# Where the second batch's q and k, the small mixing matrices U and V and the first key beacons are handled at the start of a fused attention and mixer kernel

## The chip, the cores and the metric

The kernel runs on one core of one Trainium2 chip, as one launch. The metric is the device time of that launch in microseconds (us), the median of several runs. Five engines work beside each other, each through its own list of instructions in a fixed order: TensorE (PE: matrix products and transposes, written into PSUM), VectorE (DVE), ScalarE (ACT), GpSimd (POOL) and SyncE (SP, which here only issues transfers). Transfers between memory and the core run on 16 DMA engines; the profile calls what POOL issues queue q0 and what SP issues queue q1.

## The reference, cut to what matters

Eight batches (B), eight heads (H), 576 tokens (S), 16 beacons (Nb), 64 numbers a head (D):

```python
k_all = concat([beacon_k, k]);  v_all = concat([beacon_v, v])      # 16 + 576 keys
scores = (q @ k_all.T) / 8, tokens masked causally, beacons never masked
x = softmax(scores) @ v_all                                        # heads side by side: (8, 576, 512)
u = x + (x.T @ U @ V).T                                            # U: 576 x 32, V: 32 x 576
out = u + relu(u @ w_ch1) @ w_ch2                                  # 512 -> 2048 -> 512
```

## The kernel before, in words

Attention is worked through in pairs of heads, four pairs p to a batch, 32 in all. Of each pair, q and k are turned by TensorE (`qkT_units`, lines 272 to 289: transposes into PSUM, line 260 or 266, and copies to `qT` and `kT`, lines 282 and 287), the scores are made in four column groups (`visit`, line 318, with a mask product ahead of it on line 310), ScalarE takes their exponentials (line 324), and `av_unit` (line 345) multiplies them with v; VectorE divides (lines 353 and 354) and writes `xb`. Tokens of q and k are loaded as `st` (line 192), six tokens to a partition on 96 partitions; the 16 key beacons come in on partitions 96 to 111 (lines 189 and 195). `regroup` (lines 245 to 256) copies a pair into a tile `pr`, so that one transpose serves both heads; line 255 copies the beacons beside the tokens.

When the four pairs of a batch are done, `mix_units` makes u: `head` multiplies with U (line 374, copy `qts` on line 380), `most` and `end` add the product with V (lines 410 and 422, from `Vsb` and `Vend`) to x (line 385) and write `uT` (lines 394 and 396). From then on the two big products (`g_unit`, line 449, with w1 in four loads, and `c_unit`, line 465, with w2 in two) are cut into units and slipped in between the steps of the later pairs (`fill`), until they alone are left.

The order of the start is written out by hand, and every engine keeps to it. First comes batch 0: q and k of the first pairs through SP and ACT, the rest through POOL, then `v[0]` in halves of four heads, five transfers each (line 207). Then POOL issues the lower halves (heads 0 to 3) of `k[1]` and `q[1]`, the key beacons of batch 1, the upper half of `v[0]`, and the first quarter of w1 (line 178). The rest stands in `load_rest` (lines 716 to 727), called during pair p = 0 after that turn's two transposing units: U and V are read by SP into one f32 tile `small` (three transfers of U, four of V, lines 157 to 163; a one-column memset on VectorE, line 155, stands ahead of them), POOL issues the upper halves of `k[1]` and `q[1]` and the v beacons, rounds U, V and the end of V to 16 bits (lines 167, 168 and 171), and then issues `v[1]`, the other three quarters of w1 and w2; `load_batch(2)` adds the loads of batch 2 behind them. At p = 3 the loop writes the order by hand as well (lines 750 to 755): the two `av_unit`s, the two transposing units of pair 5, `head`, and the rest of the mixing with two groups of scores (`two`, `three`) between its parts.

Every product goes through one PSUM pool of 8 buffers (line 100) that are handed round in the order of the program. `keep_warm` (line 234) multiplies constants, to keep TensorE busy: 8 products at the start (on `plain`, which lies in `Vsb`), 2 ahead of the first scores, 2 behind them (line 700), 1 further on.

Of the kernel before, what the change touches and what calls it, by code (L numbers as in the profile page):

```python
# [11 lines left out]
F32 = mybir.dt.float32  # L12
# [6 lines left out]
P = 128  # L19
# [11 lines left out]
def kernel(  # L31
# [13 lines left out]
    nc = tc.nc  # L45
    B, H, S, D = q.shape
    Nb = beacon_k.shape[2]
# [17 lines left out]
    TJ = 6  # L65
# [36 lines left out]
    def pst(shape, dtype, name):  # L102
        return psum.tile(shape, dtype, tag="ps", name=name)
# [33 lines left out]

    Vsb = const.tile([P, QM], F16, name="Vsb", tag="Vsb")
    Vend = const.tile([P, NCC, nq[NT - 1]], F16, name="Vend", tag="Vend")
    plain = Vsb[:, 0:P]  # L140
    nc.vector.memset(plain, 1.0)
    ones = const.tile([P, 1], F16, name="ones", tag="ones")
    nc.vector.memset(ones, 1.0)
# [8 lines left out]
    def small_loads():  # L152

        f = utp.tile([P, NT * R + S], F32, name="small", tag="ut")
        nc.vector.memset(f[:, 0:1], 0.0)
        uf, vf = f[:, 0 : NT * R].rearrange("p (j r) -> p j r", r=R), f[:, NT * R :]
        nc.sync.dma_start(out=uf[: nq[0], 0, :], in_=moe_U[0 : nq[0], :])
        nc.sync.dma_start(
            out=uf[:, 1 : NT - 1, :], in_=moe_U[q0[1] : QM, :].rearrange("(j p) r -> p j r", p=P)
        )  # L160
        nc.sync.dma_start(out=uf[:NL, NT - 1, :], in_=moe_U[QM:S, :])
        for cc in range(NCC):
            nc.sync.dma_start(out=vf[ds(R * cc, R), :], in_=moe_V)

        def cast():
            for rr, jj in ((nq[0], slice(0, 1)), (P, slice(1, NT - 1)), (NL, slice(NT - 1, NT))):
                nc.gpsimd.tensor_copy(out=Usb[:rr, jj, :], in_=uf[:rr, jj, :])
            nc.gpsimd.tensor_copy(out=Vsb, in_=vf[:, 0:QM])
            for cc in range(NCC):
                rs = ds(R * cc, R)  # L170
                nc.gpsimd.tensor_copy(out=Vend[rs, cc, :], in_=vf[rs, QM:S])

        return cast

    def emit_w1(i):
        w1r = moe_w_ch1.rearrange("(cc p) f -> p cc f", p=P)
        fs = ds(FF // 4 * i, FF // 4)
        nc.gpsimd.dma_start(out=w1[:, :, fs], in_=w1r[:, :, fs])
# [12 lines left out]
    def token_load(eng, src, dst, hs):  # L191
        eng.dma_start(out=dst[0:TP, hs, :], in_=src[hs].rearrange("h (p j) d -> p h (j d)", j=TJ))  # L192
# [10 lines left out]
    def v_tokens(src, vs, hs, js=range(NT)):  # L203
        dst = by_head(vs)[:, :, hs, 0:D]
        for j in js:
            a = Nb if j == 0 else 0
            nc.gpsimd.dma_start(  # L207
                out=dst[a : a + nq[j], j, :, :], in_=src[hs, ds(q0[j], nq[j]), :].rearrange("h p d -> p h d")
            )
# [5 lines left out]
    def by_token(t):  # L215
        return t.rearrange("p h (j d) -> p j h d", j=TJ)
# [17 lines left out]
    def keep_warm(ps, n, a=ident):  # L234


        w = ps.shape[-1] // P
        for _ in range(n):
            nc.tensor.matmul(
                ps[:, 0 : w * P].rearrange("p (a b) -> p a b", b=P), a,  # L240
                a.rearrange("p (a b) -> p a b", a=1).broadcast_to([P, w, P]),
                start=True, stop=True,
            )

    def regroup(st, c, i, *copies, beacons=None):

        t = pairs.tile([P, TJ, 2, D], F16, name=f"pr{i}", tag=f"pr{i}")
        src = by_token(st[i][:, 2 * c : 2 * c + 2, :])
        w = TJ // len(copies)
        for a, copy in enumerate(copies):  # L250
            js = slice(w * a, w * (a + 1))
            copy(out=t[0:TP, js], in_=src[0:TP, js])
        if i == 0:
            b = beacons if beacons is not None else src
            copies[0](out=t[TP:TB, TJ - 1], in_=b[TP:TB, TJ - 1])
        return t

    def in_pair(pr):

        return [lambda ps, o, n, j, t=t: nc.tensor.transpose(ps[:, ds(o, n)], t[:n, j, :, :], ident[:n, :n]) for t in pr]  # L260

    def by_heads(st, c):

        def turn(ps, o, n, j, t):
            for h in range(2):
                nc.tensor.transpose(  # L266
                    ps[ds(D * h, D), ds(o, n)], t[:n, 2 * c + h, ds(D * j, D)], ident[:n, :n]
                )

        return [lambda ps, o, n, j, t=t: turn(ps, o, n, j, t) for t in st]  # L270

    def qkT_units(turns, qT, kT, c, copies=((nc.vector.tensor_copy,), (nc.vector.tensor_copy,))):

        def one(i, dst, b0):
            ps = pst([P, SK], F16, name="tps")
            for j in range(TJ):
                n = TP + b0 if j == TJ - 1 else TP
                turns[i](ps, TP * j, n, j)
            w = TJ // len(copies[i])
            for a, copy in enumerate(copies[i]):  # L280
                js = slice(w * a, w * (a + 1))
                copy(  # L282
                    out=dst[:, c, b0 : b0 + S].rearrange("x (p j) -> x p j", j=TJ)[:, :, js],
                    in_=ps[:, 0:S].rearrange("x (j p) -> x p j", j=TJ)[:, :, js],
                )
            if b0:
                copies[i][-1](out=dst[:, c, 0:b0], in_=ps[:, S : S + b0])  # L287

        return [lambda: one(1, qT, 0), lambda: one(0, kT, Nb)]
# [318 lines left out]
    def qkT_of(p):  # L608
        b, c = divmod(p, NH2)
        new_qT_of(p)  # L610
        copies = [(act_copy, nc.vector.tensor_copy) if p == 0 else (nc.vector.tensor_copy,)] * 2
        turns = by_heads(Ls[b][0], c)
        for i, t in enumerate(prs.get(p, ())):
            if t is not None:
                turns[i] = in_pair(prs[p])[i]
        return qkT_units(turns, qTs[b], kTs[b % 2], c, copies)

    def scores_of(p):
# [21 lines left out]

    QUOTA = {2: 4}

    IDLE = [8, 2, 1, 0, 2]
    queue = []
    state = {"t": 0}

# [38 lines left out]
    with tc.manual_schedule(engines={ENG.PE, ENG.Activation, ENG.DVE, ENG.SP, ENG.Pool}):  # L685
# [3 lines left out]
            token_load(nc.gpsimd, src, dst, HALVES[1])  # L689
        v_beacon(beacon_v[0], vss[0])  # L690
        v_tokens(v[0], vss[0], HALVES[0])
        prs[0][0] = regroup(first, 0, 0, V, act_copy, beacons=by_token(Ls[0][0][0][:, 0:2, :]))
        keep_warm(pst([P, 512], F32, name="idle"), IDLE[0], plain)
        t0, sc = qkT_of(0), scores_of(0)
        for u in t0:
# [1 line left out]
        sc[0](IDLE[1])  # L697
        masks = sc[2]
        prs[1] = [None, regroup(first, 1, 1, V)]
        keep_warm(pst([P, 512], F32, name="idle"), IDLE[4])  # L700
        for u in qkT_of(1)[::-1]:
            u()
        clear()
# [7 lines left out]
        token_load(nc.gpsimd, q[1], qt, HALVES[0])  # L711
        key_beacons(nc.gpsimd, beacon_k[1], kt, ALLH)
        v_tokens(v[0], vss[0], HALVES[1])
        emit_w1(0)

        def load_rest():
            cast_small = small_loads()
            token_load(nc.gpsimd, k[1], kt, HALVES[1])
            token_load(nc.gpsimd, q[1], qt, HALVES[1])
            v_beacon(beacon_v[1], vss[1])  # L720
            cast_small()
            v_tokens(v[1], vss[1], HALVES[0])
            emit_w1(1)
            v_tokens(v[1], vss[1], HALVES[1])
            emit_w1(2)
            emit_w1(3)
            emit_w2()

        NP1 = NF * NH2
        for p in range(NP1):  # L730
            b, c = divmod(p, NH2)
            if c == 0 and NF <= b + 1:
                load_batch(b + 1)
            seq = []
            prior = masks
            if p + 2 < NP1:
                seq += [lambda i=i, p=p: qkT_of(p + 2)[i]() for i in range(2)]
            if NH2 + 3 <= p + 3 < NP1:
                seq.append(lambda p=p: regroup_of(p + 3))
            if p + 1 < NP1:  # L740
                one_by_one = sc[3]
                seq.append(sc[1])
                masks = sc[2]
            seq += [prior] + av_of(p)
            sc = []
            if p + 2 < NP1:
                new_qT_of(p + 2)
                sc = scores_of(p + 2)
                seq.append(lambda sc=sc, p=p: sc[0](IDLE[3] if p < NH2 else 0))
            if p == NH2 - 1:  # L750
                two, three = one_by_one
                _, head, (most, end), begin = mix_units(xbs[b], 0, False)
                seq = (
                    seq[-3:-1] + seq[0:2] + [head, two, lambda: begin([0, 1]), three, most, end] + seq[-1:]
                )
            done = 0
            for i, u in enumerate(seq):
                u()
                if p == 0 and i == 1:
                    load_rest()  # L760
                want = FIRST[p] * (i + 1) // len(seq)
                fill(want - done)
                done = want
            if c == NH2 - 1:
                if b == 0:
                    queue.extend([None] * 4)
                    feed(b)
                else:
                    mix(b)
# [146 lines left out]
```

## Time and profile before

| what | value |
|---|---|
| median of 3 runs | 358.02 us (357.6 to 358.52) |
| profiled execution, its own time | 358.65 us |
| its span, first to last instruction | 357.0 us |
| TensorE busy | 348.2 us, 98% |
| VectorE, ScalarE, GpSimd busy | 188.1, 166.1 and 97.4 us |
| mean granted TensorE clock | 0.995 |
| read from memory, written | 37.59 MB, 9.44 MB |

The profiled execution took 358.65 us, of which 357.0 us lie in the span; the 1.65 us around it are the same for any change inside. A busy TensorE is an engine with an instruction in it: where its clock is halved, the same products show longer. All that the change touches lies in the first 35 us of the span, and its transfers reach on to about 62 us.

### The profile page before, as it was taken

What the parts mean: (1) busy time and instruction counts of PE and PEld (TensorE: products, weight loads), DVE (VectorE), ACT (ScalarE), POOL (GpSimd) and SP (SyncE); (2) the same over time, 40 slices, a digit from 0 to 9 for tenths busy, and PEclk for the clock granted to TensorE, in tenths of its full rate; (3) what the DMA queues carried; (4) which work ended last, traced back from release to release, by engine and by line L of the source; (5) the groups of instructions that cost most, each with busy time, mean ns of one, the idle gap of its engine ahead of it and who ended that gap; (6) DMA issues with size and microseconds to landing.
All of it is one profiled execution on the core that took longest, in us unless ns stands there. A gap on an engine that the chain in (4) does not pass through costs nothing.

```text
span 357.0 us, 7830 instructions
## 1 busy us (share of the span) xinstructions
PE 348.2 (98%) x3134; PEld 174.1 (49%) x3134; DVE 188.1 (53%) x485; ACT 166.1 (47%) x356; POOL 97.4 (27%) x139
## 2 busy tenths in 40 slices
PE   7989999999999999999999999999999999999995
PEld 2655455455555444444444444444454444444443
DVE  5758755588986444654465447445745522313311
ACT  4966751478745464467444664556503202401400
POOL 8759613609239028304820500000000000000000
PEclk9989999999999999999999999999999999999999
DMA  8999999999999949996999893142014215115111
GB/s 171 144 177 109 188 204 175 208 173 119 107 96 140 183 98 124 156 198 86 133 147 203 129 138 80 61 101 55 31 61 99 58 59 95 25 59 90 30 55 69
DMA packets 143946, 41.37 MB, mean 116 GB/s; under 512 B 128800, under 2 KB 139296, under 8 KB 143904
## 3 DMA queue, kind: packets, MB, share of 16 engines
q0 software_dynamic: 87408, 18.18, 66.0%
q1 hardware_dynamic: 56272, 22.34, 32.1%
q8 instruction: 26, 0.43, 0.5%
q10 hardware_dynamic: 224, 0.30, 0.3%
q14 instruction: 16, 0.13, 0.1%
HBM read 37.59 MB, written 9.44 MB: 132 GB/s over the span
## 4 chain that ended last, share of the span: by engine, by line
PE 90%; DMA 4%; POOL 2%; DVE 2%; ACT 1%; issue 1%; POOLq 0%
PE gps L449 36%; PE cps L465 34%; PE po L345 8%; PE sps L318 7%; DMA vs<-in_v_dram 2%; DMA st<-in_q_dram 2%; PE tps L260 1%; PE cph L490 1%; PE qtp L374 1%; POOL vs L207 1%; PE ups L385 1%; PE ups L410 1%; POOL st L192 1%; DVE uT L392 1%; ACT expt L324 0%
## 5 line engine op out<-in xcount | busy, mean ns | idle before, releaser
L324 ACT ACTIVATE expt<-sps 128x496 f16<-128x496 f32 (+2 forms) x256 | 111.3, 533 | 63.6 <-PE sps L318 63.5
L449 PE MATMUL gps<-uT,w 128*128 128x512 f16 x576 | 135.4, 379 | 0.0
L465 PE MATMUL cps<-w,gT 128*128 128x512 f16 x560 | 132.7, 379 | 0.0
L453 ACT ACTIVATE gT<-gps 128x512 f16<-128x512 f32 x86 | 51.9, 607 | 95.0 <-PE gps L449 95.0
L449 PEld LDWEIGHTS <-w 128*128 128x128 f16 x576 | 52.0, 98 | 59.3 <-issue 3.2
L465 PEld LDWEIGHTS <-gT 128*128 128x128 f16 x560 | 49.9, 98 | 59.2 <-issue 6.8
L455 DVE TENSOR_SCALAR gT<-gps 128x512 f16<-128x512 f32 x58 | 40.0, 690 | 47.8 <-PE gps L449 46.5
L478 DVE TENSOR_TENSOR ob<-cps,ut 128x512 f32<-128x512 f32 x31 | 21.4, 690 | 49.6 <-PE cps L465 49.2
L345 PEld LDWEIGHTS <-expt 128*128 128x128 f16 (+1 forms) x960 | 37.6, 99 | 17.5 <-issue 3.8
L207 POOL DMA_DIRECT2D vs<-in_v_dram x50 | 39.6, 809 | 15.2 <-DMA w<-in_moe_w_ch_dram 8.4
L345 PE MATMUL po<-vs,expt 128*128 128x65 f16 (+1 forms) x960 | 40.5, 195 | 1.8 <-DMA vs<-in_v_dram 1.4
L318 PE MATMUL sps<-qT,kT 64*128 64x80 f16 (+4 forms) x384 | 35.0, 284 | 0.7 <-DVE kT L287 0.6
L354 DVE TENSOR_TENSOR xb<-po,rec 128x320 f16<-128x320 f32 x64 | 31.5, 492 | 2.2
L295 DVE TENSOR_TENSOR expt<-expt,bigmask 128x512 f16<-128x512 f16 x54 | 22.6, 419 | 11.7 <-ACT expt L324 11.7
L353 DVE RECIPROCAL rec<-po 128x5 f32<-128x5 f32 x64 | 12.0, 187 | 26.3 <-PE po L345 26.2
L318 PEld LDWEIGHTS <-kT 64*128 64x128 f16 x384 | 11.7, 94 | 22.7 <-issue 14.2
L189 POOL DMA_DIRECT2D vs<-in_beacon_v_dram x8 | 4.3, 532 | 59.7 <-PE po L345 59.7
L548 POOL DMA_DIRECT2D st<-in_q_dram x20 | 16.9, 864 | 3.8 <-DMA st<-in_k_dram 2.2
L548 POOL DMA_DIRECT2D st<-in_k_dram x20 | 16.9, 868 | 1.6 <-DMA vs<-in_v_dram 1.1
L392 DVE TENSOR_TENSOR uT<-ups,uT 128x496 f16<-128x496 f32 x20 | 12.1, 667 | 6.9 <-PE ups L410 3.6
L282 DVE COPY qT<-tps 128x576 f16<-128x576 f16 (+1 forms) x16 | 11.8, 736 | 3.9 <-PE tps L260 2.5
L282 DVE COPY kT<-tps 128x576 f16<-128x576 f16 (+1 forms) x16 | 11.7, 732 | 1.9 <-PE tps L266 1.1
(83 smaller groups left out, 142.2 us busy)
## 6 DMA issues: line engine op xcount, KB each, us to landing
out_dram<-ob SPq DMA_DIRECT2D x35, 256.0 KB, 2.2
vs<-in_v_dram POOLq DMA_DIRECT2D x18, 128.0 KB, 7.6
w<-in_moe_w_ch_dram POOLq DMA_DIRECT2D x4, 512.0 KB, 7.8
w<-in_moe_w_ch_dram POOLq DMA_DIRECT2D x2, 1024.0 KB, 13.6
st<-in_k_dram POOLq DMA_DIRECT2D x12, 128.0 KB, 7.5
st<-in_q_dram POOLq DMA_DIRECT2D x12, 128.0 KB, 8.9
st<-in_k_dram POOLq DMA_DIRECT2D x2, 576.0 KB, 13.1
st<-in_q_dram POOLq DMA_DIRECT2D x2, 576.0 KB, 16.0
```

What stands on the lines that cost most here:

```text
L207: nc.gpsimd.dma_start(out=dst[a : a + nq[j], j, :, :], in_=src[hs, ds(q0[j], nq[j]), :].rearrange("h p d -> p h d"))
L282: copy(out=dst[:, c, b0 : b0 + S].rearrange("x (p j) -> x p j", j=TJ)[:, :, js], in_=ps[:, 0:S].rearrange("x (j p) -> x p j", j=TJ)[:, :, js],
L295: nc.vector.tensor_tensor(out=e4, in0=e4, in1=bigmask, op=ALU.min)
L318: nc.tensor.matmul(ps[g, i][:, ds(o, w)], kT[hp, c, ds(P * ch, P)], qT[hp, c, ds(qa, w)], start=not early, stop=True, skip_group_check=early,)
L324: nc.scalar.activation(out=ex[i][:, ds(SLOT * g, gw[g])], in_=ps[g, i][:, 0 : gw[g]], func=AF.Exp, scale=scale)
L345: nc.tensor.matmul(po[:, j, :], ex[0 : nk[c], ds(blk[(c, j)], P)], vs[0 : nk[c], ds(c * H * E + h * E, E)], start=(c == 0), stop=(c == j),)
L354: nc.vector.tensor_tensor(out=xb[:, :, ds(h * D, D)], in0=po[:, :, 0:D], in1=r.broadcast_to([P, NT, D]), op=ALU.mult)
L449: nc.tensor.matmul(g[:, 0:n], w1[:, cc, ts(dc, P)], uT[:, cc, ds(t0, n)], start=(cc == 0), stop=(cc == NCC - 1))
L453: nc.scalar.activation(out=gT["t"][:, dc, 0:n], in_=g[:, 0:n], func=AF.Relu)
L455: nc.vector.tensor_scalar_max(out=gT["t"][:, dc, 0:n], in0=g[:, 0:n], scalar1=0.0)
L465: nc.tensor.matmul(ps[:m, :], gT["t"][:, dc, ds(P * i, m)], w2[:, dc, :], start=(dc == 0), stop=turned and dc == NDC - 1, skip_group_check ...
L548: nc.gpsimd.dma_start(out=dst[a : m[j], j, :, :], in_=src[:, ds(q0[j], nq[j]), :].rearrange("h p d -> p h d"))
```

## The change

It does five things.

1. POOL issues the upper halves of `k[1]` and `q[1]` ahead of the first quarter of w1, outside `load_rest`.
2. `load_rest` is called one pair later, at p = 1. For POOL this alters nothing of the order by itself; the memset that SP's reads of U and V wait for stands one pair later on VectorE. POOL rounds U and V straight away, ahead of the v beacons of batch 1.
3. The four small copies that round the end of V (`cast_end`) leave POOL and are made by VectorE, at p = 3, between the second `av_unit` and the transposing units of pair 5.
4. The key beacons of the first pair are no longer copied beside the tokens: `beacons_apart` turns the 96 tokens as before and the 16 beacons by two small transposes straight from `st`.
5. The two `keep_warm` products of line 700 go, and `plain` lies in `w2` instead of `Vsb`.

```diff
-    plain = Vsb[:, 0:P]
+    plain = w2[:, 0, 0:P]
...
             nc.gpsimd.tensor_copy(out=Vsb, in_=vf[:, 0:QM])
+
+        def cast_end():
             for cc in range(NCC):
                 rs = ds(R * cc, R)
-                nc.gpsimd.tensor_copy(out=Vend[rs, cc, :], in_=vf[rs, QM:S])
-
-        return cast
+                nc.vector.tensor_copy(out=Vend[rs, cc, :], in_=vf[rs, QM:S])
+
+        return cast, cast_end
...
-        if i == 0:
-            b = beacons if beacons is not None else src
-            copies[0](out=t[TP:TB, TJ - 1], in_=b[TP:TB, TJ - 1])
+        if i == 0 and beacons:
+            copies[0](out=t[TP:TB, TJ - 1], in_=src[TP:TB, TJ - 1])
...
+    def beacons_apart(turn, st, c):
+
+        def both(ps, o, n, j):
+            turn(ps, o, TP, j)
+            for h in range(2) if n > TP else ():
+                nc.tensor.transpose(
+                    ps[ds(D * h, D), ds(o + TP, Nb)], st[TP:TB, 2 * c + h, ds(D * j, D)], ident[TP:TB, TP:TB],
+                )
+
+        return both
...
+        if p == 0:
+            turns[0] = beacons_apart(turns[0], Ls[0][0][0], 0)
...
-        keep_warm(pst([P, 512], F32, name="idle"), IDLE[4])
...
         v_tokens(v[0], vss[0], HALVES[1])
+        token_load(nc.gpsimd, k[1], kt, HALVES[1])
+        token_load(nc.gpsimd, q[1], qt, HALVES[1])
         emit_w1(0)
 
         def load_rest():
-            cast_small = small_loads()
-            token_load(nc.gpsimd, k[1], kt, HALVES[1])
-            token_load(nc.gpsimd, q[1], qt, HALVES[1])
+            cast, cast_end = small_loads()
+            cast()
             v_beacon(beacon_v[1], vss[1])
-            cast_small()
             v_tokens(v[1], vss[1], HALVES[0])
             emit_w1(1)
...
             emit_w2()
+            return cast_end
...
-                    seq[-3:-1] + seq[0:2] + [head, two, lambda: begin([0, 1]), three, most, end] + seq[-1:]
+                    seq[-3:-1] + [cast_end] + seq[0:2] + [head, two, lambda: begin([0, 1]), three, most, end] + seq[-1:]
...
-                if p == 0 and i == 1:
-                    load_rest()
+                if p == 1 and i == 1:
+                    cast_end = load_rest()
```

More of the change, by code (lines that the diff above doesn't have):

```diff
@@ L243, in keep_warm, with regroup @@
             )
-    def regroup(st, c, i, *copies, beacons=None):
+    def regroup(st, c, i, *copies, beacons=True):
         t = pairs.tile([P, TJ, 2, D], F16, name=f"pr{i}", tag=f"pr{i}")
@@ L641 @@
     QUOTA = {2: 4}
-    IDLE = [8, 2, 1, 0, 2]
+    IDLE = [8, 2, 1, 0]
     queue = []
@@ L691 @@
         v_tokens(v[0], vss[0], HALVES[0])
-        prs[0][0] = regroup(first, 0, 0, V, act_copy, beacons=by_token(Ls[0][0][0][:, 0:2, :]))
+        prs[0][0] = regroup(first, 0, 0, V, act_copy, beacons=False)
         keep_warm(pst([P, 512], F32, name="idle"), IDLE[0], plain)
```

## The prediction

> **What bounds the kernel now.** The page comes first: PE is busy 98% of the span and fills 90% of the chain that ended last. So the time is PE's work plus PE's stops, and the only long stop is early. The chain in order of time shows it:
>
> ```profile
> PE 90%; DMA 4%; POOL 2%; DVE 2%; ACT 1%; issue 1%; POOLq 0%
> ```
>
> ```profile
> 4.49 6.63 DMA st<-in_q_dram
> ...
> 12.60 2.90 POOL vs L207 x4
> 15.50 6.99 DMA vs<-in_v_dram
> 22.53 1.03 PE po L345 x16
> ```
>
> PE at 22.53 starts on v[0]'s upper half, whose last transfer was issued at 15.50 and took 6.99 us. The table by stage shows the stop and what followed:
>
> ```profile
> 20.00:22.00 2.00, 1.12 (x23) 0.78 (x23) 0.74 (x3) 2.00 (x6) 0.96 (x4) 1.00 1.20 215
> 22.00:24.00 2.00, 1.47 (x22) 1.27 (x23) 1.05 (x4) 0.11 (x1) 0.00 (x0) 0.61 1.29 218
> 24.00:26.00 2.00, 2.00 (x28) 1.22 (x27) 0.47 (x2) 1.42 (x4) 1.27 (x4) 0.53 1.02 149
> 26.00:28.00 2.00, 1.92 (x62) 1.46 (x60) 1.93 (x6) 0.54 (x2) 1.94 (x5) 1.00 0.37 45
> ```
>
> The columns are the stretch, the busy time of PE, PEld, DVE, ACT and POOL, the granted clock, the DMA share and GB/s. After the stop the clock is down (0.61, then 0.53) until about 26. At 26 to 28 the DMA engines, full until then, fall to 45 GB/s: POOL had stood still for V and then rounded it. The timeline has these rows:
>
> ```profile
> 13.68 0.06 DVE L155 MEMSET small<- 128x1 f32 x1
> ...
> 15.14 2.86 SPq L163 DMA_DIRECT2D small<-in_moe_V_dram  x4
> ...
> 18.47 0.68 POOL L192 DMA_DIRECT2D st<-in_k_dram  x1 [1.55 <-DMA st<-in_q_dram]
> ...
> 24.61 0.60 POOL L168 CAST Vsb<-small 128x496 f16<-128x496 f32 x1 [3.43 <-PE sps L318]
> ...
> 25.16 1.17 POOL L171 CAST Vend<-small 32x80 f16<-32x80 f32 x4
> ...
> 26.28 3.59 POOL L207 DMA_DIRECT2D vs<-in_v_dram  x5
> ...
> 29.64 0.39 PE L410 MATMUL ups<-Vsb,qts 32*128 32x496 f16 x4
> ```
>
> The row of Vsb names PE, but the transfer list has V's last transfer issued at 17.58 and landing after:
>
> ```profile
> small<-in_moe_V_dram SPq DMA_DIRECT2D x1, 72.0 KB, 6.9
> ```
>
> 17.58 + 6.9 = 24.5: POOL waited for V. I call V's landing T; before, T = 24.5. Behind it on POOL stand v[1], w1, w2 and batch 2. Its last trace is here, where a copy waits 0.89 for batch 2's key beacons:
>
> ```profile
> 60.96 0.19 DVE L255 COPY pr<-st 16x128 f16<-16x128 f16 x1 [0.89 <-DMA st<-in_beacon_k_dram]
> ```
>
> **The change, part by part.**
>
> *Beacon copy and keep-warm products.* The copy (DVE, 5.90 to 6.41) goes; PE had waited for it and finished the first k at 6.69. Without it the 96-row transposes end by 6.32, plus two small ones at 37 ns (12 of 96 rows took 0.45): 6.4. That is 0.25 earlier for the first exponentials (8.34). The two products are 0.53 of PE (8.45 to 8.98). But ACT runs on without a break to 22.1, so of both only ACT's gap before 10.45 (0.15) and the 0.25 come through: **0.4**. No wait is added: those beacons landed at 1.44 + 4.0 = 5.4. Bounds: 0 (hidden by the wait for v) to 0.8. `plain`'s new place costs nothing: w2 is written from 37 on, the products end at 4.8.
>
> *U and V a slot later.* v[0]'s upper half no longer shares the DMA engines with them. Its last transfer took 7.0; the same transfer of the lower half (issued at 8.67, no U and V beside it) took 5.4. So it lands up to 1.6 sooner (bounds 0 and 1.6), at 20.9, about when PE, 0.4 ahead, wants it. Worth: av of pair 2 then costs 1.09 (the row of pair 1) and not 20.37 to 23.37, 1.9 less; what PE did from 23.37 to 26.3 at half clock (0.59, 0.98, 1.55) costs about 1.0 less at the full clock. With the 0.4, PE ends av of pair 3 at 23.0 and not 26.3: **3.3 won, if nothing is late next.**
>
> *V is late next.* The new memset stands behind pair 3's copies (17.39 before, 17.0 now). V's last issue came 3.9 after the memset, so at 20.9. Latencies of these seven reads were 5.5 to 6.9 with the DMA share above 1; it stays so, as k[1], q[1] and w1 (landed 26.0, 27.4 and 24.7 before) are still to come. So T = 26.4 to 27.8; I take **27.3**, near the upper end because q[1] and w1 are both in flight then. The bounds are wider: 22.5 (a read alone on SP took 3.1 to 4.4 in the first microseconds, less something) and 28.5.
>
> *Who waits for T.* Three chains, each against its row:
>
> - VectorE. `cast_end` waits for T, and behind it in order stand the q and k copies of pair 5 (0.75, 0.75, 0.15) and `qts` (0.28). The four copies have no row on DVE: 0.155 (128x16) to 0.51 (the 16x128 copy, beside POOL) each, so 0.6 to 2.0; I take 0.19, the 80x80 row, 0.75. PSUM's 8 buffers let PE get no further than `three` meanwhile. So L410 comes at T + 0.1 + 0.75 + 1.65 + 0.28 + 0.3 = T + 3.1 = 30.4 (before: 29.64), **0.8 late**.
> - v[1], first half. POOL rounds Vsb (T + 0.1 to T + 0.7), issues the v beacons (0.54) and starts v[1] at T + 1.24; the fifth issue lies 2.92 on and took 2.7 to land: T + 6.9 = 34.2. Its first reader's last product ended at 33.18: with T = 27.3 it ends at about 34.2, **1.0 late**; it breaks even at T = 26.1 (some product time lies behind the landing). The 1.17 of Vend and POOL's place for the v beacons are in this: without them v[1] had started at T + 1.8.
> - Batch 2. The DMA engines are full from 32 to 61, so whatever POOL issues later lands later by as much. v[1] starts at 28.54 for 26.28: 2.26 later; the copy at 60.96 moves with it. Its q and k are done at 62.85 and PE turned them at 63.35, so 0.5 is spare: **1.8 late**. In between w1 and w2 have more room (the second quarter of w1 lands at 36.7, its first product is at 38.66; the last of w2 lands at 54.0, needed at 56.6).
>
> They overlap; the largest sets the end: **+1.8**. The 3.3 is spent in waiting. *k[1] and q[1] ahead of w1* cost nothing: w1's first quarter landed at 24.7, its first product is at 33.0, and 5 us of later landing are covered; if that cover went, PE would stop for what is over. The two were wanted at 31 and had landed at 27.4.
>
> The sum: span 357.0 + 1.8 = 358.8, own time 360.4 for 358.65. The runs' median, 358.02, lies 0.63 below the profiled run, so the prediction is 358.02 + 1.8 = **359.8**.
>
> **A rule that speaks against this.** The DMA engines carried U and V beside POOL's backlog at 5.5 to 6.9 us each. The Trainium skill (DMA: Bandwidth & Descriptors, Queues, rings and completion order) says each engine takes turns between the queues that have work, a packet at a time; by that alone a read from SP need not wait for POOL's backlog. By it V would land as it does unhindered; that is the rival called V early. The trace's latencies of 5.5 to 6.9 us are against it.
>
> **The rivals.**
>
> - *V early (faster).* If V takes the 3.5 of the first reads (3.1 to 4.4), T = 20.9 + 3.5 = 24.4. Then batch 2 is 24.4 + 1.24 - 26.28 - 0.5 = -1.1, the other chains are earlier still: **356.9**; at T = 22.5 it is -3.0, 355.0. It decides from T below 25.5. For it: the early rows, and less v to carry. Against it: the seven latencies, and that k[1], q[1] and w1 are unfinished. I give T below 24.9 two in ten, centre 356.5.
> - *A draw.* T of 24.9 to 26.4, through a share of both: -0.6 to +0.9, about **358.2**.
> - *The clock as well (slower still).* PE in the new order has little from 26.0 (two groups of scores done) to 28.8 (the first copy, which frees a buffer). Before, 1.7 us with 0.3 of work halved the clock for some 3.4. If that comes after 29, the 2.9 between L410 and av of pair 4 grow by up to 1.7: 0.8 + 1.7 = +2.5, **360.5**; with T = 28, 361.2. The Trainium skill (TensorE: Matmul & The Clock Gate, Why this matters for your kernels) bids one avoid idle gaps over about 3 us. By that a gap of 2.8 would cost nothing; the stop of 1.7 in this trace did cost.
> - *It doesn't do what it says.* q[1]'s lower half, not U and V, holds v[0] up, and the stop at 21 stays. Then PE is at cast_end at 26, T is the same, and the time too: **359.8**, with the clock's dip where it was.
>
> **How the numbers follow.** Forecast (with the last rival) 0.5; V early 0.2; draw 0.2; clock as well 0.1. The likeliest gives 359.8. Its own range is T = 26.4 to 27.8 by the batch-2 chain, 358.9 to 360.3, and 2.0 for slow copies carries the VectorE chain to +2.0. The range of 8 in 10 leaves out the lower half of V early and the worst of the clock: **356.3 to 361.4**. A measurement can tell about 0.3% here, 1.07 us. Faster than 356.95: most of V early, 0.16. Within: the draw, the rest of V early and the forecast's lowest T, 0.27. Slower than 359.09: 0.57.
>
> **What would show it.** Right: PE's wait for v[0] at 21 short; VectorE's first 32x80 copy waiting for `small` until about 27; Vsb's row at 27.4; v[1] starting near 28.5; L410 near 30.4; the beacon copy of batch 2 near 63. Wrong: V landing by 25, then all of these come early and the end with them; or the DMA engines falling idle before 26, which would say that V had no backlog to wait for. It is wrong in size if the four copies take over 1.2, or if the clock is low after 26.

## The result, and the profile after

The changed kernel takes **360.28 us** (median of 6 runs, 359.74 to 361.26); the kernel before, run beside it, 357.76 (6 runs, 356.91 to 358.52). The ratio is **1.0078, with a 95% interval of 1.0056 to 1.0100**: slower by 0.8%, 2.5 us by the medians, where 1.8 was forecast. Ratios here are taken over runs within 1.5% of their kernel's fastest, so they can differ a little from the medians.

The profiled execution of the changed kernel took 359.74 us, the shortest of its six, with a span of 358.1 for 357.0. It shows the way in which the time went, but not all of it: 1.1 of some 2.5 us. Lines of code stand up to 14 higher than before (`av_unit` is L357, the first big product L461).

The chain that ended last has changed its make-up:

```profile
PE 81%; DMA 10%; DVE 3%; POOL 2%; SPq 1%; ACT 1%; issue 1%; ACTq 0%; POOLq 0%
```

PE's share falls from 90% to 81%, and DMA's rises from 4% to 10%: transfers now end waits for longer. More than half of that 10% is one transfer, the key beacons of batch 2 (20.49 us); the last part shows that it did not add to the time. The timeline says which waits matter (start, duration, engine and line; in brackets the idle time ahead and what ended it):

```profile
17.52 0.06 DVE L155 MEMSET small<- 128x1 f32 x1
...
18.98 2.56 SPq L163 DMA_DIRECT2D small<-in_moe_V_dram  x4
...
20.55 1.09 PE L357 MATMUL po<-vs,expt 128*128 128x65 f16 x30
...
25.00 0.32 PE L267 MATMUL tps<-ident,st 96*64 96x96 f16 x5 [1.08 <-issue]
...
26.67 0.20 DVE L173 CAST Vend<-small 32x80 f16<-32x80 f32 x1 [0.19 <-DMA small<-in_moe_V_dram]
...
26.80 0.60 POOL L168 CAST Vsb<-small 128x496 f16<-128x496 f32 x1 [1.78 <-DMA small<-in_moe_V_dram]
...
27.87 3.58 POOL L209 DMA_DIRECT2D vs<-in_v_dram  x5
...
29.13 0.60 PE L422 MATMUL ups<-Vsb,qts 32*128 32x496 f16 x4
...
33.04 1.01 PE L357 MATMUL po<-vs,expt 128*128 128x65 f16 x15
...
33.86 1.16 PE L461 MATMUL gps<-uT,w 128*128 128x512 f16 x4
```

In the kernel before, the first big product stood here:

```profile
33.02 1.03 PE L449 MATMUL gps<-uT,w 128*128 128x512 f16 x4
```

The stop of TensorE at 21 is gone: the 30 products of pair 2 take 1.09. But V, read 3.84 us later, lands about 2.2 later, near 26.7 (24.5 before). VectorE's last small copy waits for it, and so does POOL, which starts v[1] at 27.87 for 26.28. The first of the big products comes at 33.86 for 33.02. From there on PE is busy again and nothing is made good. In this trace TensorE never waits for v[1] itself: the row at 33.04, which reads it, has no wait. TensorE even reads V at 29.13, 0.51 ahead of the kernel before (29.64), but then takes 4.73 us to the first big product where it took 3.38.

The table by stage (stretch; busy time of PE, PEld, DVE, ACT and POOL; granted clock; DMA share; GB/s) shows why:

```profile
24.00:26.00 2.00, 1.00 (x31) 0.74 (x33) 0.68 (x3) 0.21 (x1) 0.21 (x1) 1.00 1.09 221
26.00:28.00 2.00, 1.22 (x19) 0.80 (x18) 1.49 (x4) 1.06 (x2) 1.21 (x3) 0.83 0.22 38
28.00:30.00 2.00, 2.00 (x20) 1.20 (x21) 0.80 (x4) 0.82 (x3) 2.00 (x3) 0.50 0.59 38
30.00:32.00 2.00, 2.00 (x30) 1.10 (x29) 1.49 (x4) 1.88 (x5) 2.00 (x4) 0.50 1.15 73
```

TensorE is busy for little more than half of 24 to 28, and runs at half clock from 27.3 to 34.1; before, the half clock stood at 22 to 26. The DMA engines carry 38 GB/s from 26 to 30: POOL, which waits for U and V, issues no transfer between the first quarter of w1 (18.52) and the v beacons (27.34).

### The profile page after: what moved, and what is told of

It reads as the page before. It is cut to its first block, busy times and chain, and to the rows that moved or that the text cites. A ratio compares the mean times of both kernels' runs of the same rounds, so it can differ in the third digit from the quotient of the medians.

```text
span 358.1 us, 7829 instructions
## 1 busy us (share of the span) xinstructions
PE 350.0 (98%) x3134; PEld 175.2 (49%) x3134; DVE 188.5 (53%) x488; ACT 166.4 (46%) x356; POOL 96.3 (27%) x135
## 4 chain that ended last, share of the span: by engine, by line
PE 81%; DMA 10%; DVE 3%; POOL 2%; SPq 1%; ACT 1%; issue 1%; ACTq 0%; POOLq 0%
PE cps L477 32%; PE gps L461 31%; PE sps L330 7%; PE po L357 6%; DMA st<-in_beacon_k_dram 6%; DMA w<-in_moe_w_ch_dram 2%; DMA small<-in_moe_V_dram 2%; PE tps L261 1%; DMA stk<-in_k_dram 1%; POOL vs L209 1%; PE cph L502 1%; ACT expt L336 1%; PE qtp L386 1%; DVE pr L254 1%; PE ups L422 1%; DVE uT L404 1%
## 5 line engine op out<-in xcount | busy, mean ns | idle before, releaser
L461 PE MATMUL gps<-uT,w 128*128 128x512 f16 x576 | 135.5, 380 | 0.0
L461 PEld LDWEIGHTS <-w 128*128 128x128 f16 x576 | 52.1, 98 | 59.4 <-issue 3.4
L357 PEld LDWEIGHTS <-expt 128*128 128x128 f16 (+1 forms) x960 | 36.8, 98 | 15.2 <-issue 1.9
L357 PE MATMUL po<-vs,expt 128*128 128x65 f16 (+1 forms) x960 | 39.6, 195 | 0.2 <-DVE ob L490 0.2
```

The source lines that it names most:

```text
L357: nc.tensor.matmul(po[:, j, :], ex[0 : nk[c], ds(blk[(c, j)], P)], vs[0 : nk[c], ds(c * H * E + h * E, E)], start=(c == 0), stop=(c == j),)
L461: nc.tensor.matmul(g[:, 0:n], w1[:, cc, ts(dc, P)], uT[:, cc, ds(t0, n)], start=(cc == 0), stop=(cc == NCC - 1))
```

## The experiments

Each kernel was timed in 5 rounds beside the kernel before; ratios are to that kernel. Where an edit is given it is made to the changed kernel, unless it says otherwise. All of them compute the whole result.

### Undoing one part at a time

**The slot.** U and V are read at pair 0 again.

```diff
-                if p == 1 and i == 1:
+                if p == 0 and i == 1:
                     cast_end = load_rest()
```

> Theory A (V lands late because its reads wait a slot longer; TensorE then stops at pair 3, the clock halves, and POOL starts v[1] 1.6 us later than before): with the reads of U and V back at pair 0 and all else as changed, V lands near 24.5, v[1] starts near 25.8, and the time is 357.3 to 358.5. Rival 1 (the four copies of V's end hold VectorE up, whenever V lands): 359.5 or more. Rivals 2 (the order of k[1], q[1] and w1) and 3 (the start: no beacon copy, two products fewer, a clock that comes up later): 360.3 as it is.

Measured: 357.99 us, ratio 1.0002 (0.9976 to 1.0028). The slot is the whole loss: undone alone, it takes all of it back. Its trace:

```profile
24.09 1.02 DVE L173 CAST Vend<-small 32x80 f16<-32x80 f32 x4
...
24.85 3.59 POOL L209 DMA_DIRECT2D vs<-in_v_dram  x5
...
25.66 0.32 PE L267 MATMUL tps<-ident,st 96*64 96x96 f16 x5 [1.86 <-issue]
```

VectorE's four copies wait for nothing, and v[1] starts at 24.85, 1.4 ahead of the kernel before. TensorE does not stop at 21 here either. What that wins is lost in a stop of 1.86 with no releaser, after which the clock is halved for some 3.4 us; the first big product is at 32.97, as before the change (33.02).

**The end of V.** It goes back to POOL, behind `Vsb`.

```diff
             nc.gpsimd.tensor_copy(out=Vsb, in_=vf[:, 0:QM])
-
-        def cast_end():
             for cc in range(NCC):
                 rs = ds(R * cc, R)
-                nc.vector.tensor_copy(out=Vend[rs, cc, :], in_=vf[rs, QM:S])
+                nc.gpsimd.tensor_copy(out=Vend[rs, cc, :], in_=vf[rs, QM:S])
+
+        def cast_end():
+            pass
```

> The end of V goes back to POOL, all else as changed. Theory A: v[1] starts 1.2 us later still, 360.3 to 361.5. Rival 1: VectorE is free at pair 3, 358 to 359. Rivals 2 and 3: 360.3.

Measured: 362.58 us, 1.0147 (1.0111 to 1.0183), slower still, and above the range of theory A too: in this trace v[1] starts 1.9 us later than in the changed kernel, not 1.2. The trace shows the link to v[1] in the open (here `av_unit` is L358, the big product L462):

```profile
29.77 3.59 POOL L210 DMA_DIRECT2D vs<-in_v_dram  x5
...
33.59 0.25 PE L358 MATMUL po<-vs,expt 128*128 128x65 f16 x3 [0.92 <-DMA vs<-in_v_dram]
...
34.20 0.28 PE L358 MATMUL po<-vs,expt 128*128 128x65 f16 x4 [0.36 <-DMA vs<-in_v_dram]
...
35.52 0.49 PE L358 MATMUL po<-vs,expt 128*128 128x65 f16 x6 [1.03 <-DMA vs<-in_v_dram]
35.82 1.90 PE L462 MATMUL gps<-uT,w 128*128 128x512 f16 x4
```

VectorE is free, so TensorE reaches pair 4 early, and waits there three times for v[1], block by block. In the same trace the DMA engines move nothing at all at 28 to 30:

```profile
28.00:30.00 2.00, 1.56 (x18) 1.00 0.00 0
```

(stretch, busy PE, clock, DMA share, GB/s). POOL has waited for V until 27.59 and then rounds it, with every further load behind it. Rival 1 falls: moving the end of V to VectorE was the better place for it.

**The order of k[1], q[1] and w1.**

```diff
-        token_load(nc.gpsimd, k[1], kt, HALVES[1])
-        token_load(nc.gpsimd, q[1], qt, HALVES[1])
         emit_w1(0)
...
             cast, cast_end = small_loads()
+            token_load(nc.gpsimd, k[1], kt, HALVES[1])
+            token_load(nc.gpsimd, q[1], qt, HALVES[1])
             cast()
```

> The upper halves of k[1] and q[1] go back behind the first quarter of w1, all else as changed. Theory A: V still lands near 26.7, 359.8 to 360.8. Rival 2: 357.8 to 358.8. Rivals 1 and 3: 360.3.

Measured: 360.75 us, 1.0098 (1.0066 to 1.0129). No gain; the order costs nothing that can be measured, as forecast. Rival 2 falls.

**The start.** The beacon copy and the two constant products come back.

```diff
-        if p == 0:
-            turns[0] = beacons_apart(turns[0], Ls[0][0][0], 0)
...
-        prs[0][0] = regroup(first, 0, 0, V, act_copy, beacons=False)
+        prs[0][0] = regroup(first, 0, 0, V, act_copy, beacons=None)
...
         prs[1] = [None, regroup(first, 1, 1, V)]
+        keep_warm(pst([P, 512], F32, name="idle"), 2)
```

(and in `regroup`, as before, the copy of the beacons).

> The beacon copy and the two keep-warm products come back, all else as changed. Theory A: 359.8 to 360.9. Rival 3: the clock is full before 6 us again and the time 357.8 to 358.8. Rivals 1 and 2: 360.3.

Measured: 361.11 us, 1.0099 (1.0061 to 1.0138). Rival 3 falls. Nor does the new start win anything that shows.

**The slot alone, in the kernel before.** Only the call of `load_rest` is moved, in the kernel before.

```diff
-                if p == 0 and i == 1:
+                if p == 1 and i == 1:
                     load_rest()
```

> The kernel before with nothing changed but load_rest one pair later, so U and V alone are read later. Theory A (the slot is the whole cost): V lands near 28, v[1] starts near 29.8, 360.5 to 363. If it takes the slot and the other edits together: 357.8 to 359.

Measured: 361.98 us, 1.0109 (1.0074 to 1.0143). Without any of the other edits the slot costs as much. So in the kernel before the later slot alone makes the loss, as in the changed kernel undoing it alone takes the loss away. VectorE has none of V's copies here; POOL's queue is enough. v[1] starts at 28.81 in this trace, the first big product is at 34.41.

### By which way a late V costs

**The clock.** Eight constant products stand ahead of the stop at pair 3.

```diff
-            [lambda: visit([2]), lambda: visit([3])],
+            [lambda: visit([2]), lambda idle=0: visit([3], idle)],
...
-    [head, two, lambda: begin([0, 1]), three, most, end]
+    [head, two, lambda: begin([0, 1]), lambda: three(8), most, end]
```

> As changed, with 8 constant products (1.7 us at full clock) ahead of TensorE's stop at pair 3, so that its clock should stay up after 27. Theory A1 (of the late V it is the halved clock that costs): 358.8 to 359.8. Theory A2 (POOL's late start of v[1] sets the end, through batch 2's beacons): 360.0 to 361.0.

Measured: 361.06 us, 1.0086 (1.0055 to 1.0117): no gain, and just above A2's range. Yet the products did what they were for:

```profile
30.00:32.00 2.00, 2.00 (x28) 1.00 0.90 57
32.00:34.00 2.00, 1.77 (x42) 1.00 1.42 88
```

The clock is full where it was halved, and TensorE arrives at pair 4 only to wait for v[1]:

```profile
34.72 0.40 PE L357 MATMUL po<-vs,expt 128*128 128x65 f16 x6 [0.71 <-DMA vs<-in_v_dram]
34.95 1.03 PE L461 MATMUL gps<-uT,w 128*128 128x512 f16 x4
```

So A1 falls as the whole cause: beside so late a v[1], a full clock only brings TensorE to the next wait. With v[1] early it wasn't tried, so what the half clock costs there stays open. A2 named the right queue but, as below, not the right reader.

**VectorE's place alone.** The four copies stand just ahead of the products that read V.

```diff
-    seq[-3:-1] + [cast_end] + seq[0:2] + [head, two, lambda: begin([0, 1]), three, most, end]
+    seq[-3:-1] + seq[0:2] + [head, two, lambda: begin([0, 1]), three, cast_end, most, end]
```

> As changed, but the four copies of V's end stand behind VectorE's other work of pair 3, just ahead of the products that read V. TensorE then goes on at 25 and stops less. If VectorE's place in line costs (the first of the prediction's three chains): 358.5 to 359.5. Theory A2 (POOL): 360.0 to 360.8, for v[1] starts no sooner.

Measured: 362.39 us, 1.0118 (1.0074 to 1.0162): no gain, and above both ranges. VectorE no longer waits with other work behind it, but POOL does, and TensorE's waits for v[1] add up to

```profile
PE po L357 <- DMA vs<-in_v_dram: 2.3, 4, 0.9
```

(us in total, times, longest).

**POOL's place alone.** The lower half of v[1] goes ahead of the rounding.

```diff
-            cast()
             v_beacon(beacon_v[1], vss[1])
             v_tokens(v[1], vss[1], HALVES[0])
+            cast()
```

> As changed, but POOL issues the beacons and the lower half of v[1] ahead of rounding U and V. Theory A2: batch 2 no longer comes late, 358 to 359.3. Theory A1: V lands later still beside v[1], the stop at pair 3 grows, 360.3 to 361.5.

Measured: 360.56 us, 1.0080 (1.0051 to 1.0109): no gain either. v[1] starts at 19.80, and batch 2's beacon copy comes at 60.57, earlier than before the change; so A2, which ran through batch 2, falls. Now VectorE is the one that waits, and TensorE behind it:

```profile
27.01 0.50 DVE L173 CAST Vend<-small 32x80 f16<-32x80 f32 x2 [0.30 <-DMA small<-in_moe_V_dram]
27.43 0.60 POOL L168 CAST Vsb<-small 128x496 f16<-128x496 f32 x1 [2.95 <-DMA small<-in_moe_V_dram]
27.54 0.76 DVE L294 COPY qT<-tps 128x576 f16<-128x576 f16 x1
...
28.35 0.22 PE L322 MATMUL sps<-negmask,identb 128*128 128x128 bf16 x1 [1.87 <-DVE qT L294]
```

The time lies in A1's range, and the clock is halved from 28.6 to 32.0; with v[1] early, the wait and the half clock behind it can't be told apart here.

Two queues wait for V side by side, then. That each hides what freeing the other would give became theory C.

**Both places.** The last two edits together, V still read a slot late.

> As changed, with U and V still read a slot later, but neither queue waits for V with other work behind it: POOL issues the lower half of v[1] ahead of rounding, and VectorE rounds V's end behind its other work of pair 3. If the late V costs only through these two queues (theory C, from the traces so far: the first big product comes 5.6 to 6.1 us after POOL starts v[1], and freeing one queue alone leaves the other): 357.5 to 359. If V's lateness costs by itself, whoever waits (theory D: the product that reads V is late): 360 or more.

Measured: 358.49 us, 1.0023 (0.9990 to 1.0055), against 1.0078 for the changed kernel. Theory C holds: with nothing behind V in either queue, most of the loss is gone although V is no sooner. By the medians 0.74 us is left, which the interval doesn't tell from nothing. The profiled execution of this kernel is one of its longest (360.67 us), with U itself late: TensorE stops for 1.70 with no releaser and waits 1.43 for U, V is rounded at 29.45, and the first big product comes at 34.91. So a late U or V can still cost, as theory D has it; how often it does so here isn't shown.

### Towards a version that beats both

The remaining three read U and V at pair 0 or earlier.

**The slot undone and VectorE's copies late** (the edits of the first and of `cast_end`).

> U and V read at pair 0 again, and V's end rounded behind VectorE's other work; the rest as changed. Theory C: POOL starts v[1] near 25, TensorE's stop at pair 3 shrinks, 355.8 to 357.2. If the stop is TensorE's own (theory E: the earlier trace showed 1.9 us with no releaser ahead of the pair's last five transposes): 357.5 to 358.3, as with the slot alone undone.

Measured: 357.51 us, 0.9988 (0.9955 to 1.0020). The profiled execution has a span of 354.9, its clock full from 5.3 on and the first big product at 30.75, 2.3 ahead of the kernel before; over twelve runs (355.59 to 359.83) that does not come every time. The median lies at the lower edge of theory E's range, the profiled execution (356.66) in theory C's; between the two it stays unclear.

**With v[1] ahead of the rounding as well.**

> The same with the lower half of v[1] issued ahead of rounding. Theory C: 355.3 to 357. Theory E: 357.5 to 358.3. If v[1] beside V slows V down by over 2 us: 358 to 359.5.

Measured: 357.91 us, 0.9988 (0.9956 to 1.0020). No more than the one above, and in theory E's range, not C's. But in this trace TensorE waits 1.7 for v[0] at 20, which neither theory has.

**U and V earlier still.** The reads start ahead of batch 1's loads.

```diff
+        cast, cast_end = small_loads()
         Ls[1] = qk_tiles()
         (kt, qt), _ = Ls[1]
...
         def load_rest():
-            cast, cast_end = small_loads()
             cast()
```

(on top of the slot undone and the copies late; POOL rounds V at its place in line).

> As the second, with the reads of U and V earlier still, from about 11.4, ahead of batch 1. V lands near 22, but beside the lower halves of k[1] and q[1] and the upper half of v[0]. Theory C: if TensorE then waits for v[0] at 21 as before the change, 357 to 358.5; if not, 355.5 to 357.

Measured: 356.89 us, 0.9973 (0.9942 to 1.0003). It has the lowest median of all, 0.86 under the 357.75 of the kernel before, but its interval still takes in 1: a lead that these runs don't prove. The memset stands at 10.05, V is rounded at 20.80 without a wait, and v[1] starts at 21.87. TensorE doesn't wait for v[0] at 21, but now it waits for its lower half, 1.2 us in all up to 14.6, and the clock is halved from 14.1 to 17.5: in part the earlier reads have only moved the stop forward.

## Why the prediction was right, point by point

- **V is late next: right.** Forecast: memset at 17.0, last issue at 20.9, V at 27.3. Measured: 17.52, 20.48 and about 26.7 in the changed kernel; its four reads took 6.1 to 6.4 us (5.5 to 6.9 forecast). In the other kernels with the late slot VectorE's or POOL's last wait for V ended between 26.9 and 29.5. The rule of the Trainium skill (DMA: Bandwidth & Descriptors, Queues, rings and completion order), by which engines take turns between queues, did not save V: 72 KB took over 6 us beside POOL's backlog. V early and the draw didn't come.
- **U: no term, and not always free.** POOL waits for U first, and `head` reads it. In the trace of the changed kernel TensorE doesn't wait for it, but in five of the eight others with the late slot it does, for 0.4 to 1.6 us. No run tells U's part from V's.
- **The stop at 21: right.** v[0]'s last transfer was issued at 15.31 and took 5.4 us: 20.7, forecast 20.9, and TensorE didn't wait. It ended pair 3's products near 23.4 (forecast 23.0). The gain was real, and was spent by the next wait.
- **The start: wrong, 0.4 forecast and nothing seen.** The first exponential came at 8.32 (8.34 before), and ACT's unbroken run at 10.77 (10.45). In this execution TensorE ran at half speed there, up to about 10 us (the four products of the first scores took 0.98 us, 0.58 before); the copy's 0.25 doesn't show through. Putting the old start back didn't change the time.
- **VectorE's chain: the wait came, its lateness didn't.** The copies took 0.19 to 0.20 each, as taken; L410's successor, L422, came at 29.13 with V at 26.7: V + 2.5, forecast V + 3.1. That the first three copies were done as their own transfers landed made it 0.6 shorter. That is 0.51 ahead of the kernel before, where 0.8 late was forecast: what the wait cost in this trace came behind it, through the clock (below).
- **v[1]'s chain: right, too small.** The forecast had v[1] start at V + 1.24; it was 27.87 with V at 26.7. In the seven kernels with the late slot where POOL waited, the first big product came 5.6 to 6.1 after that start (5.99 here, 6.05, 5.75, 6.12, 6.06, 5.98, 5.60). With the forecast's own 28.54 this gives 34.5, 1.5 late and not 1.0: the products behind the last landing were counted too low. In five of the seven TensorE is seen to wait for v[1]. In the changed kernel's own trace and in that of the old order it isn't; there the half clock, to 34.1 and 34.9, brought it no sooner, so that these two fit the 6 us by chance as far as is known.
- **Batch 2's chain: the step that failed.** It was called the largest, at +1.8, and it cost nothing. Its copy did come late, even by 2.37 for the 2.26 forecast:

```profile
63.33 0.19 DVE L256 COPY pr<-st 16x128 f16<-16x128 f16 x1 [2.17 <-DMA st<-in_beacon_k_dram]
...
66.79 0.58 PE L330 MATMUL sps<-qT,kT 64*128 64x496 f16 x4
```

  In the kernel before:

```profile
61.18 0.88 DVE L252 COPY pr<-st 96x768 f16<-96x768 f16 x2
...
63.35 0.42 PE L260 MATMUL tps<-ident,pr 96*128 96x96 f16 x6
...
65.83 0.58 PE L318 MATMUL sps<-qT,kT 64*128 64x496 f16 x4
```

  But the scores behind it came at 66.79 for 65.83: 0.96 late, hardly more than the 0.84 that TensorE had brought along from 33.86, and it was 0.97 late already at its last product ahead of pair 8 that needs none of this (L485, 63.23 for 62.26). The mistake lay in the spare time: the copies up to 62.85 were taken for pair 8's, and the later ones are pair 9's. Pair 8's were done near 61.5 and read at 63.35, so 1.8 was spare and not 0.5. The chain of waits in the profile after runs through this very transfer (20.49 us of it): a chain with no slack left, not one that added time.
- **The clock as well: came, and is part of it.** It was halved from 27.3 to 34.1 in this trace, and here it made the lateness of the first big product: 4.73 us from the product that reads V, for 3.38. Kept full beside a late v[1], the time was the same, since TensorE then waited for v[1]; so the half clock alone isn't the cause, and its share in the changed kernel stays open. Where the half clock reached beyond the first big product it cost more: in the kernel before with the late slot, 1.39 late at the first big product became 2.96 at the scores of pair 8, with the clock halved from 35.3 to 38.8. Three others show the same (the end of V on POOL, the old start, VectorE's place alone), each with 1.2 to 1.4 more; in the other five with the late slot it was 0.12 at most. The Trainium skill (TensorE: Matmul & The Clock Gate, Why this matters for your kernels) warns of gaps over about 3 us; here a stretch of 4 us with TensorE half busy was enough.
- **The sum.** The forecast of 359.8 lies 0.5 under the measured 360.3. That it came so near is luck in part, for its size came from the chain that cost nothing. The runs put the loss on the two chains that were put at 0.8 and 1.0, and each alone was enough to keep it. The profiled execution has 1.1 of the 2.5. A later V, at 27 to 28 as in most of the other traces, or a half clock beyond the first big product would give the rest in a typical run, but no trace of such a run of the changed kernel is at hand.

**What stays open.** How the loss divides between the wait for V, the wait for U and the half clock was not measured apart. And the stop ahead of pair 5's last five transposes (1.08 here, 1.86, 1.4 and 1.7 in three others, 0.3 or nothing in the rest) falls on the same instruction each time, and the profile names no releaser. In each a 16 KB transfer of the "instruction" queue ended some 1.3 to 1.5 us before the transposes went on, in the midst of the full DMA engines. The Trainium skill (Runtime: NRT & Kernel Launch, Instruction fetch mechanics) says that an engine streams its instructions through a DMA queue of its own, and that this is mostly hidden; that it is not hidden here is a guess, and wasn't tried.

## What to carry to other kernels

A load that is put off gains for what it stood in the way of and loses for what waits for it: look up who waits, on every engine's queue, and what stands behind each. Where two queues wait for the same transfer, freeing one can show nothing; free both before you call the transfer innocent. And count the spare time of a chain with the instruction that reads it, since neighbouring copies on the same line may belong to the next tile.

## What the runs showed of the hardware

- Transfers that SP issues take long while POOL keeps the DMA engines full: 72 KB of V took 6.1 to 6.4 us in the changed kernel, where 144 KB read by SP at the very start took 2.8 and 3.4. So do writes: the first three of 256 KB, near 60 us, took 5.8 in the median, the seven of the last 58 us 2.0.
- The clock at the start differs from one execution to the next. The two constant products ahead of the first scores took 0.60 us before the change and 1.03 in the changed kernel, with nearly the same instructions ahead of them. In the trace with the old start put back the clock also came up only near 10 us, and in eight others with the new start between 3.9 and 5.3: the change is not what sets it.
- One queue of POOL that waits for 72 KB and then rounds it left the 16 DMA engines without any work for 2 us (the second undoing above), early in a kernel that moves 41 MB.
